# The last half step of a two-stage attention kernel: scalings and copies shared with VectorE, last output tile stored from two queues

## The chip, the cores and the metric

The kernel runs on one core of a Trainium2 chip, as one launch. The metric is the device time of a whole execution in microseconds. Of the core's engines, TensorE (PE) multiplies and transposes, VectorE (DVE), ScalarE (ACT) and GpSimd (POOL) work on tiles in SBUF and PSUM, and SyncE (SP) issues the transfers to and from DRAM, which 16 DMA engines carry out.

## The reference

Two attentions follow each other. The first is a causal window attention of 8 batches, 8 heads, 576 positions and 64 dimensions, with a window of 64. Its output, as 576 rows of 512 per batch, goes into a mixture of 4 attention experts: a gate picks the best two of four experts for every row, each expert has its own query, key, value and output weights, and the outputs are added with the gate's weights.

```python
# stage 1, per batch and head
mask = (rel >= 0) & (rel < window)
scores = np.where(mask, scale * q @ k.T, -1e9)
x = softmax(scores) @ v                        # then heads side by side: x is (8, 576, 512)
# stage 2, for each of 4 experts
q, k, v = x @ wq[e], x @ wk[e], x @ wv[e]      # 512 -> 64
a = softmax(causal(q @ k.T / 8))
ye = a @ v @ wo[e]                             # 64 -> 512
out += mask[..., None] * w[:, :, kk:kk + 1] * ye   # only where e is among the row's best two
```

## The kernel before

Stage 1 works in groups of four 64-row blocks for a pair of heads; stage 2 works per batch b on a pair pr of experts at a time. One (b, pr) is a half step, and there are 16 of them; the two stages overlap, so that stage 2 of a batch runs while stage 1 works on later batches. A list of calls, each with a due time from a table of positions, is sorted by that time and executed in this order when the program is written. For due times from 1.0 to 15.5 TensorE's order is that of the list; behind that, where the last half steps lie, a scheduler orders TensorE's instructions by when their inputs are expected. The instructions of the other engines follow in the order that the scheduler gives them; each engine then works through its own list, and waits on semaphores for the others.

A half step of stage 2 goes like this. TensorE makes the scores, VectorE takes a masked minimum (L471), ScalarE the exponentials (L475). `s2_w` multiplies the unnormalised probabilities by gate weight over row sum: three short VectorE operations (L506 to L508) give a factor for each of nine tiles x = 0 to 8, and GpSimd multiplies the tiles (L512). Tile 0 is `px` (64 columns); tiles 1 to 8 have 192, 192, 320, 320, 448, 448, 576 and 576 columns. Tiles 1 to 4 lie in the buffer named p_0 in the profile; 5 to 8 in p_1 or p_2, depending on pr (p_2 in the last half step). `s2_t` transposes 128-column pieces on TensorE, four to a PSUM tile of the tag "t" (three buffers), in two parts: part 0 from p_0 (k = 0, 1, 2) and part 1 from p_1 or p_2 (k = 0 to 3). In the names of such tiles, t_7_1_0_1 is b = 7, pr = 1, part 0, k = 1. Copies on ScalarE (L528 to L561) bring them into pt_0 or pt_1. `s2_av_mm` multiplies them with the values (L580) into another PSUM tile of the same tag, o_7_1_0 or o_7_1_1, in 36 or 20 products. `s2_av_out` splits the result into a high part yh (ScalarE, L591) and a rest yl (VectorE, L592). `s2_o` multiplies those of both pairs with the output weights: `three` (L340 to L342) is called for each pair, six matmuls of 512 columns for one of five output tiles ops_0 to ops_4 of a batch.

The last step of `s2_o` is the one that ends the program: VectorE copies a tile of 128 x 512 from PSUM into an SBUF tile "out" (two buffers) at L601, and SyncE stores it (L603). The ninth block of 64 rows of an even batch is kept until the odd batch after it: tile j = 4 holds 64 rows of each and is stored by two transfers of 64 rows (L606).

Of the kernel before, what the change touches and what calls it, by code (L numbers as in the profile page):

```python
# [11 lines left out]
AF = mybir.ActivationFunctionType  # L12
OP = mybir.AluOpType
# [3 lines left out]
NB, NH, S, D = 8, 8, 576, 64  # L17
# [22 lines left out]
def window_attention_moe_attention(ctx: ExitStack, tc: tile.TileContext, qT, kT, vW,  # L40
                                   wg, wq, wk, wv, wo, out):
    nc = tc.nc
# [69 lines left out]
    for h in range(2):  # L112
        r = slice(64 * h, 64 * h + 64)
# [12 lines left out]
    for h in range(2):  # L126
        r = slice(64 * h, 64 * h + 64)
        for x in range(2):
            c = slice(64 * x, 64 * x + 64)
# [168 lines left out]
    def row(i, e):  # L298

        return (0, 0, 384, 0, 896)[i] + e * (64 + 128 * i)  # L300

    def chunk(i, e, c):

        if e == 0:
            return row(i, 0) + 128 * c
        return row(i, 1) + 64 + 128 * (i - 1 - c)
# [32 lines left out]
    def three(ps, ah, al, bh, bl, first, last):  # L339
        nc.tensor.matmul(ps, lhsT=ah, rhs=bh, start=first, stop=False)  # L340
        nc.tensor.matmul(ps, lhsT=ah, rhs=bl, start=False, stop=False)  # L341
        nc.tensor.matmul(ps, lhsT=al, rhs=bh, start=False, stop=last)  # L342
# [120 lines left out]
    def s2_soft(b, pr, k):  # L463
# [26 lines left out]
        if k == 1:  # L490
            least(banks[0][:, 448:512], PX[0][:, 0], m_f[:, 1, 64:128], r2[:, 0, 0:1])
            exp(PX[0][:, 0], 0)
            s2_w(b, pr, 0)
        if k == 3:
            nc.vector.tensor_tensor(r2[:, 0, 7:9], m2[:, :, 0], m2[:, :, 1], op=OP.min)  # L495
            for e in range(2):
                exp(P2S[pr][1][:, row(4, e):row(4, e) + 576], 7 + e)
            if pr or b % 2:
                s2_w(b, pr, 1)

    def s2_w(b, pr, k):

        x0, x1 = ((0, 7), (7, 9))[k]
        r2 = R2[b, pr]
        x = slice(x0, x1)
        nc.vector.tensor_scalar_add(r2[:, 2, x], r2[:, 1, x], 1e-9)  # L506
        nc.vector.reciprocal(r2[:, 2, x], r2[:, 2, x])
        nc.vector.tensor_mul(r2[:, 3, x], r2[:, 2, x], G2[b % 2][:, pr, x])  # L508
        for x in range(x0, x1):
            i, e = (x + 1) // 2, (x + 1) % 2  # L510
            p = PX[0][:, 0] if x == 0 else P2S[pr][i > 2][:, row(i, e):row(i, e) + 64 + 128 * i]
            nc.gpsimd.tensor_scalar(p, p, r2[:, 3, x:x + 1], 1.0, op0=OP.mult, op1=OP.mult)  # L512

    def s2_t(b, pr, part, k):
        ps = psum.tile([128, 512], F32, tag="t", bufs=3, name=f"t2_{b}_{pr}_{part}_{k}")
        pt = PT2[part]

        def one(col, i, e, c):

            at = chunk(i, e, c) if c < i else row(i, 1) - 64  # L520
            nc.tensor.transpose(ps[:, col:col + 128], P2S[pr][part][:, at:at + 128], ident)  # L521

        def odd(col, col0):
            for e in range(2):
                r = slice(64 * e, 64 * e + 64)
                dst = pt[r, e, col0:col0 + 256].rearrange("r (a c) -> r a c", c=64)[:, 0:4:3]
                src = ps[r, col:col + 256].rearrange("r (a c) -> r a c", c=64)[:, 1::2]
                nc.scalar.activation(dst, src, AF.Copy)  # L528

        if part == 0 and k == 0:  # L530
            for e in range(2):
                for i in (1, 2):
                    one(256 * e + 128 * i - 128, i, e, 0)
            nc.scalar.activation(pt[:, :, 64:320], ps.rearrange("r (e c) -> r e c", e=2), AF.Copy)
        elif part == 0 and k == 1:
            for e in range(2):
                one(128 * e, 2, e, 1)
            one(256, 1, 0, 1)
            one(384, 2, 0, 2)
            nc.scalar.activation(pt[:, :, 384:512], ps[:, 0:256].rearrange("r (e c) -> r e c", e=2), AF.Copy)  # L540
            odd(256, 320)
        elif part == 0:
            nc.tensor.transpose(ps[:, 0:128], PX[0].rearrange("r a c -> r (a c)"), ident)
            for e in range(2):
                nc.scalar.activation(pt[64 * e:64 * e + 64, e, 0:64], ps[0:64, 64 * e:64 * e + 64], AF.Copy)
        elif k < 2:
            for c in range(2):
                for i in (3, 4):
                    one(256 * c + 128 * i - 384, i, k, c)
            nc.scalar.activation(pt[:, k, 0:512], ps, AF.Copy)  # L550
        elif k == 2:
            for e in range(2):
                for i in (3, 4):
                    one(256 * e + 128 * i - 384, i, e, 2)
            nc.scalar.activation(pt[:, :, 512:768], ps.rearrange("r (e c) -> r e c", e=2), AF.Copy)
        else:
            for e in range(2):
                one(128 * e, 4, e, 3)
            one(256, 3, 0, 3)
            one(384, 4, 0, 4)  # L560
            nc.scalar.activation(pt[:, :, 832:960], ps[:, 0:256].rearrange("r (e c) -> r e c", e=2), AF.Copy)  # L561
            odd(256, 768)

    def y_col(b, blk):

        return 64 * blk + 64 * (b % 2 == 1 and blk == BLK - 1)
# [27 lines left out]
    def s2_o(b, j):  # L594
        ps = psum.tile([128, DM], F32, tag="s", bufs=5, name=f"ops_{b}_{j}")
        for pr in range(2):
            y0 = y_col(b, 2 * j) if j < 4 else 512
            yh, yl = (y[pr][:, y0:y0 + 128] for y in (YH, YL))
            three(ps, yh, yl, whi["o"][:, pr], wlo["o"][:, pr], pr == 0, pr == 1)
        t = work.tile([128, DM], F32, tag="out", bufs=2, name=f"out_{b}_{j}")  # L600
        nc.vector.tensor_copy(t, ps)  # L601
        if j < 4:
            nc.sync.dma_start(out[b, 128 * j:128 * j + 128], t)  # L603
        else:
            for i in range(2):
                nc.sync.dma_start(out[b - 1 + i, 512:576], t[64 * i:64 * i + 64])  # L606

    def half(n):

        it = []  # L610

        def spread(key, calls):
            lo, hi = POS[key + "e" if n >= 2 * NB else key]
            for i, (f, *args) in enumerate(calls):
                it.append((n + lo + (hi - lo) * (i + 0.5) / len(calls), f, args))

        b, pr = (n - 1) // 2, (n - 1) % 2
        zb, zp = (n - 2) // 2, n % 2
        if 0 <= zb < NB and n >= 2:
            late = "l" if zp == 0 and zb % 2 == 0 and MERGE else str(zp)  # L620
            spread("T0" + str(zp), [(s2_t, zb, zp, 0, k) for k in range(3)])
            spread("T1" + late, [(s2_t, zb, zp, 1, k) for k in range(4)])
            if late == "l":
                spread("VT", [(s2_v, zb, 4), (s2_gate, zb, 4, 5), (s2_w, zb, 0, 1)])
            if zp == 1:
                spread("O0", [(s2_o, zb, j) for j in range(2)])
                spread("O1", [(s2_o, zb, j) for j in range(2, 4 + zb % 2)])
        if n >= 1 and b < NB:
            if pr == 0:
                spread("KQ1", [(f, b, 1, h) for h in range(2) for f in (s2_k, s2_q)])  # L630
        if n % 2 == 0 and n // 2 < NB:
            b = n // 2
            spread("V", [(s2_v, b, j) for j in range(5 - MERGE)])
            spread("G", [(s2_gate, b, 0, 4)])
            spread("KQ0", [(f, b, 0, h) for h in range(2) for f in (s2_k, s2_q)])
        return it
# [26 lines left out]
    for g in range(NG1):  # L663
        t = (g - LEAD) / 4.5 + LAG[0]
# [4 lines left out]
        b, k = g // 9, g % 9  # L669
# [72 lines left out]
```

## Time and profile before

| | us |
|---|---|
| three executions | 493.12, 493.98, 496.29 |
| median | 493.98 |
| the profiled execution | 494.57 |
| its span, first to last instruction | 492.5 |
| TensorE busy in it | 475.6 |
| VectorE / ScalarE / GpSimd busy | 391.5 / 345.4 / 201.0 |

In the profile a row of a group names the line, the engine, the operation and out<-in. Buffer numbers are left out there. A chain of waits is followed back from the last instruction: each piece has its start, its length and what ran. "issue" is time for which the profile shows no cause, and names such as DVEq and SPq are the engines' own instruction queues. The windows give busy times between two moments, with the share in which the 16 DMA engines moved data.

### The profile page before, as it was taken

The page shows a single profiled execution, that of the slowest core. Times are in us where ns is not written, and L with a number is a line of the kernel's source. Part 1 is how long each engine was busy: PE and PEld are TensorE (multiplying, and loading weights), DVE is VectorE, ACT ScalarE, POOL GpSimd, SP SyncE. Part 2 cuts the span into 40 slices and gives each one's busy share as a digit, 9 for nine tenths or more (in the row PEclk, how much of TensorE's full clock was granted, in tenths as well). Part 3 has the DMA queues.
Part 4 walks back from the last instruction along what each step waited for, and adds up shares of the span by engine and source line. Part 5 has one row for each costly group of instructions (what it writes and reads, how often), then busy time and mean ns, then how long its engine had stood idle before and what let it go on. Part 6 is the DMA issues. An engine that isn't in the chain of part 4 may idle for free. (4 is left out here: it accounts for less than half of the span.)

```text
span 492.5 us, 14853 instructions
## 1 busy us (share of the span) xinstructions
PE 475.6 (97%) x5132; PEld 443.6 (90%) x5132; DVE 391.5 (79%) x1820; ACT 345.4 (70%) x1365; POOL 201.0 (41%) x545
## 2 busy tenths in 40 slices
PE   5899999999999999999999999999999999999995
PEld 5789999899999999999999999999999999898874
DVE  6767879789978898888987899788997886655533
ACT  5989788677676765858577776667768685556480
POOL 7647254633444262542536243263345413242130
PEclk9999999999999999999999999999999999999999
DMA  8995252321433343223433214433152100200103
GB/s 299 320 217 149 83 158 92 101 78 65 150 94 100 111 129 126 68 77 121 165 101 100 75 70 149 116 100 101 54 169 65 50 23 24 64 3 23 65 1 107
DMA packets 49754, 51.28 MB, mean 104 GB/s; under 512 B 35472, under 2 KB 35984, under 8 KB 49680
## 3 DMA queue, kind: packets, MB, share of 16 engines
q1 hardware_dynamic: 49680, 50.35, 33.3%
q8 instruction: 40, 0.66, 0.6%
q14 instruction: 34, 0.28, 0.2%
HBM read 40.90 MB, written 9.44 MB: 102 GB/s over the span
## 5 line engine op out<-in xcount | busy, mean ns | idle before, releaser
L475 ACT ACTIVATE p<-p,r 128x192 f32<-128x192 f32 (+3 forms) x128 | 77.3, 605 | 47.4 <-DVE r L495 30.8
L512 POOL TENSOR_SCALAR p<-p,r 128x192 f32<-128x192 f32 (+3 forms) x128 | 74.6, 601 | 80.0 <-DVE r L508 50.2
L205 POOL TENSOR_SCALAR p<-p,st 128x64 f32<-128x64 f32 x216 | 65.4, 325 | 64.3 <-PE o L266 19.3
L182 PE MATMUL s<-k,qbd 128*128 128x128 f32 (+1 forms) x540 | 74.6, 284 | 7.9 <-POOL qbd L94 5.7
L200 ACT ACTIVATE p<-p,st 128x64 f32<-128x64 f32 x216 | 72.4, 338 | 13.7 <-DVE p L198 5.9
L182 PEld LDWEIGHTS s<-k,qbd 128*128 128x128 f32 x540 | 68.6, 197 | 10.8 <-POOL qbd L94 5.7
L238 DVE TENSOR_TENSOR pt<-t,tri 64x512 f32<-64x512 f32 (+1 forms) x120 | 76.0, 633 | 2.2
L193 DVE CUSTOM_DVE_ANT_0 sm<-s,win 128x128 f32<-128x128 f32 x264 | 65.3, 284 | 7.5 <-PE s L182 4.5
L471 DVE CUSTOM_DVE_ANT_0 p<-s,causal 128x320 f32<-128x320 f32 (+3 forms) x160 | 66.6, 472 | 0.6
L521 PE MATMUL t<-ident,p 128*128 128x128 f32 x384 | 52.3, 273 | 0.3 <-POOL p L512 0.2
L580 PE MATMUL o<-pt,v 128*64 128x128 f32 (+3 forms) x896 | 49.9, 263 | 0.0
L580 PEld LDWEIGHTS o<-pt,v 128*64 128x64 f32 x896 | 45.3, 137 | 1.7 <-ACT pt L528 0.4
L521 PEld LDWEIGHTS t<-ident,p 128*128 128x128 f32 x384 | 44.0, 141 | 2.1 <-POOL p L512 0.7
L456 PE MATMUL s<-kt,qt 64*128 64x256 f32 (+2 forms) x480 | 44.3, 321 | 0.1
L266 PE MATMUL o<-pt,v 128*64 128x64 f32 x1152 | 41.3, 225 | 1.0 <-ACT pt L227 1.0
L266 PEld LDWEIGHTS o<-pt,v 128*64 128x64 f32 x1152 | 36.5, 138 | 6.1 <-ACT pt L227 1.6
L340 PE MATMUL kps<-xh,wkhi 128*128 128x320 f32 (+1 forms) x128 | 39.3, 307 | 1.7 <-DVE m L471 1.7
L200 ACT ACTIVATION_READ_ACCUMULATOR p<-p,st 128x1 f32 x216 | 40.9, 189 | 0.0
L340 PE MATMUL qps<-xh,wqhi 128*128 128x320 f32 (+1 forms) x128 | 39.9, 311 | 0.0
L340 PE MATMUL v2ps<-wvhi,xh 128*128 128x260 f32 x128 | 38.9, 304 | 0.0
L361 POOL TENSOR_SCALAR v<-vo 64x128 f32<-64x128 f32 x64 | 19.2, 301 | 47.8 <-ACT vo L359 31.7
L456 PEld LDWEIGHTS s<-kt,qt 64*128 64x128 f32 x480 | 34.5, 185 | 4.5 <-DVE r L471 0.5
(141 smaller groups left out, 1238.9 us busy)
## 6 DMA issues: line engine op xcount, KB each, us to landing
v<-in_vW_dram SPq DMA_DIRECT2D x32, 576.0 KB, 5.2
k<-in_kT_dram SPq DMA_DIRECT2D x30, 320.0 KB, 3.9
out_dram<-out SPq DMA_DIRECT2D x32, 256.0 KB, 2.0
qbd<-in_qT_dram SPq DMA_DIRECT2D x56, 144.0 KB, 3.3
out_dram<-out SPq DMA_DIRECT2D x8, 128.0 KB, 2.4
p<-in_kT_dram SPq DMA_DIRECT2D x2, 320.0 KB, 7.3
q<-in_qT_dram SPq DMA_DIRECT2D x2, 288.0 KB, 3.4
p<-in_qT_dram SPq DMA_DIRECT2D x2, 288.0 KB, 7.1
```

The lines of the kernel that those rows point to most:

```text
L182: nc.tensor.matmul(ps[:, i, c:], lhsT=qbd_buf[p % 2][:, b], rhs=pairs[p][1][:, 64 * b + c:64 * b + 128], start=True, stop=True)
L200: nc.scalar.activation(pt[:, i], pt[:, i], AF.Exp, bias=st[:, 0, i:i + 1], scale=-1.0, accum_out=st[:, 1, i:i + 1])
L205: (nc.vector if g < FIRST and i < 1 else nc.gpsimd).tensor_scalar(pt[:, i], pt[:, i], st[:, 2, i:i + 1], 1.0, op0=OP.mult, op1=OP.mult)
L238: nc.vector.tensor_mul(t[64 * w:64 * w + 64, :n, e], ps[r, :n], tri[r, w, None, :].to_broadcast([64, n, 128]))
L266: nc.tensor.matmul(o[64 * h:64 * h + 64, 4 * (k % 2) + i], lhsT=pairs[p][2][:, h, b], rhs=t[:, i, 64 * h:64 * h + 64], start=True, stop=True)
L340: nc.tensor.matmul(ps, lhsT=ah, rhs=bh, start=first, stop=False)
L456: nc.tensor.matmul(banks[e][:, at(i, e):at(i, e) + n], lhsT=QT[pr][r, w, q], rhs=rhs, start=x == 0, stop=x == 2)
L471: nc.vector.tensor_tensor_reduce(out=dst, in0=ps, in1=mask, scale=1.0, scalar=3.0e38, op0=OP.add, op1=OP.min, accum_out=to)
L475: nc.scalar.activation(p, p, AF.Exp, bias=r2[:, 0, x:x + 1], scale=-1.0, accum_out=r2[:, 1, x:x + 1])
L512: nc.gpsimd.tensor_scalar(p, p, r2[:, 3, x:x + 1], 1.0, op0=OP.mult, op1=OP.mult)
L521: nc.tensor.transpose(ps[:, col:col + 128], P2S[pr][part][:, at:at + 128], ident)
L580: nc.tensor.matmul(o[64 * h:64 * h + 64, q0:q0 + w], lhsT=V2[b % 2][:, c, 2 * pr + h], rhs=PT2[part][:, h, x:x + w], start=a == 0, stop=a ...
```

## The change

In the last half step alone, (b, pr) = (7, 1), the tiles with odd x (1, 3, 5 and 7) are scaled by VectorE and not by GpSimd, and the copies of transposes with odd k (k = 1 and 3) are made by VectorE and not by ScalarE, through a helper `copy`. The last output tile (b = 7, j = 4) is copied in two halves of 256 columns: ScalarE takes columns 0 to 255 and issues their store from its own queue, VectorE takes columns 256 to 511 and SyncE issues their store. Each of the two stores covers both batches in one transfer, with a destination of 2 x 64 x 256. Before, each of the two covered one batch with 64 x 512. Lines below the change move by up to 14: L512 is L513 after, L580 is L587, L591 and L592 are L598 and L599, L601 is L615; all copies of transposes have the helper's lines, L521 on VectorE and L523 on ScalarE.

```diff
         for x in range(x0, x1):
...
-            nc.gpsimd.tensor_scalar(p, p, r2[:, 3, x:x + 1], 1.0, op0=OP.mult, op1=OP.mult)
+            engine = nc.vector if (b, pr) == (NB - 1, 1) and x % 2 else nc.gpsimd
+            engine.tensor_scalar(p, p, r2[:, 3, x:x + 1], 1.0, op0=OP.mult, op1=OP.mult)

     def s2_t(b, pr, part, k):
...
+        def copy(dst, src):
+            if (b, pr) == (NB - 1, 1) and k % 2:
+                nc.vector.tensor_copy(dst, src)
+            else:
+                nc.scalar.activation(dst, src, AF.Copy)
+
...
-                nc.scalar.activation(dst, src, AF.Copy)
+                copy(dst, src)
...
-            nc.scalar.activation(pt[:, :, 832:960], ps[:, 0:256].rearrange("r (e c) -> r e c", e=2), AF.Copy)
+            copy(pt[:, :, 832:960], ps[:, 0:256].rearrange("r (e c) -> r e c", e=2))
             odd(256, 768)
...
         t = work.tile([128, DM], F32, tag="out", bufs=2, name=f"out_{b}_{j}")
+        if b == NB - 1 and j == 4:
+            rows = out[b - 1:b + 1, 512:576]
+            nc.scalar.activation(t[:, 0:256], ps[:, 0:256], AF.Copy)
+            nc.scalar.dma_start(rows[:, :, 0:256], t[:, 0:256])
+            nc.vector.tensor_copy(t[:, 256:512], ps[:, 256:512])
+            nc.sync.dma_start(rows[:, :, 256:512], t[:, 256:512])
+            return
         nc.vector.tensor_copy(t, ps)
         if j < 4:
             nc.sync.dma_start(out[b, 128 * j:128 * j + 128], t)
```

How the orders move is shown at three places. The first is VectorE at the last half step's scalings, before; r is the tile of factors, yl the rest of the output of the attention.

```order
1756 L508 TENSOR_TENSOR r_7_1_7750<-r_7_1_7750,g_1_143 128x7
1757 L506 TENSOR_SCALAR r_7_1_7750<-r_7_1_7750 128x2
1758 L507 RECIPROCAL r_7_1_7750<-r_7_1_7750 128x2
1759 L508 TENSOR_TENSOR r_7_1_7750<-r_7_1_7750,g_1_143 128x2
1760 L592 TENSOR_TENSOR yl_138<-o_7_0_1_7848,yh_136 128x192
1761 L592 TENSOR_TENSOR yl_138<-o_7_0_1_7848,yh_136 128x64
1762 L592 TENSOR_TENSOR yl_139<-o_7_1_0_7871,yh_137 128x320
1763 L601 COPY out_0_7940<-ops_0_7933 128x512
```

And after:

```order
1756 L508 TENSOR_TENSOR r_7_1_7750<-r_7_1_7750,g_1_143 128x7
1757 L513 TENSOR_SCALAR p_0_69<-p_0_69,r_7_1_7750 128x192
1758 L513 TENSOR_SCALAR p_0_69<-p_0_69,r_7_1_7750 128x320
1759 L513 TENSOR_SCALAR p_2_71<-p_2_71,r_7_1_7750 128x448
1760 L521 COPY pt_0_130<-t_7_1_0_1_7834 128x2x128
1761 L521 COPY pt_0_130<-t_7_1_0_1_7834 64x2x64 x2
1762 L506 TENSOR_SCALAR r_7_1_7750<-r_7_1_7750 128x2
1763 L507 RECIPROCAL r_7_1_7750<-r_7_1_7750 128x2
1764 L508 TENSOR_TENSOR r_7_1_7750<-r_7_1_7750,g_1_143 128x2
1765 L513 TENSOR_SCALAR p_2_71<-p_2_71,r_7_1_7750 128x576
1766 L599 TENSOR_TENSOR yl_138<-o_7_0_1_7848,yh_136 128x192
```

The scalings of tiles 1, 3 and 5 (L513) and the copies of t_7_1_0_1 (L521) now stand between the factors for the first seven tiles and those for the last two (L506 to L508).

The second place is TensorE around the last attention products, before (o_7_1_1, L580, is the product of part 1; ops_1 and ops_2 are output tiles):

```order
2383 L342 MATMUL ops_0_7933<-wohi,yl_139 128x512
2384 L340 MATMUL ops_1_7943<-wohi,yh_137 128x512
2385 L580 MATMUL o_7_1_1_7910<-pt_1_131,v_1_145 64x64 x2
2386 L580 MATMUL o_7_1_1_7910<-pt_1_131,v_1_145 64x96 x2
2387 L580 MATMUL o_7_1_1_7910<-pt_1_131,v_1_145 64x128 x12
2388 L580 MATMUL o_7_1_1_7910<-pt_1_131,v_1_145 64x96 x2
2389 L341 MATMUL ops_1_7943<-wolo,yh_137 128x512
2390 L342 MATMUL ops_1_7943<-wohi,yl_139 128x512
2391 L340 MATMUL ops_2_7953<-wohi,yh_136 128x512
```

And after:

```order
2383 L342 MATMUL ops_0_7933<-wohi,yl_139 128x512
2384 L340 MATMUL ops_1_7943<-wohi,yh_137 128x512
2385 L341 MATMUL ops_1_7943<-wolo,yh_137 128x512
2386 L587 MATMUL o_7_1_1_7910<-pt_1_131,v_1_145 64x64
2387 L342 MATMUL ops_1_7943<-wohi,yl_139 128x512
2388 L587 MATMUL o_7_1_1_7910<-pt_1_131,v_1_145 64x64
2389 L587 MATMUL o_7_1_1_7910<-pt_1_131,v_1_145 64x96 x2
2390 L587 MATMUL o_7_1_1_7910<-pt_1_131,v_1_145 64x128 x12
2391 L587 MATMUL o_7_1_1_7910<-pt_1_131,v_1_145 64x96 x2
2392 L340 MATMUL ops_2_7953<-wohi,yh_136 128x512
```

The last two matmuls of ops_1 stood behind the products of o_7_1_1; now L341 stands ahead of them and L342 behind the first of them.

The third place is the end of the program with what each instruction waits for. VectorE before:

```order
1772 L601 COPY out_1_7950<-ops_1_7943 128x512 [waits DMAHW2_49,PE_49]
1773 L592 TENSOR_TENSOR yl_139<-o_7_1_1_7910,yh_137 128x64 [waits Activation_49]
1774 L601 COPY out_2_7960<-ops_2_7953 128x512 [waits DMAHW3_49,PE_49]
1775 L601 COPY out_3_7970<-ops_3_7963 128x512 [waits DMAHW4_49,DVE_49,PE_49]
1776 L601 COPY out_4_7980<-ops_4_7973 128x512 [waits DMAHW5_49,DVE_49,PE_49]
```

After, the end of ScalarE's list:

```order
704 L523 ACTIVATE pt_1_131<-t_7_1_1_2_7896 128x2x256 [waits PE_49]
705 L598 ACTIVATE yh_137<-o_7_1_1_7910 128x192 [waits PE_49]
706 L598 ACTIVATE yh_137<-o_7_1_1_7910 128x64 [waits DVE_49]
707 L610 ACTIVATE out_4_7980<-ops_4_7973 128x256 [waits DMAHW3_49,DMAHW4_49,DMAHW2_49,DMAHW5_49,DMAHW1_49,DMAHW6_49,DMAHW0_49,DMAHW7_49,DVE_49,PE_49]
708 L611 DMA out_dram<-out_4_7980 2x64x256 [waits Activation_49]
```

And the end of VectorE's list after:

```order
1781 L599 TENSOR_TENSOR yl_139<-o_7_1_1_7910,yh_137 128x192 [waits Activation_49]
1782 L599 TENSOR_TENSOR yl_139<-o_7_1_1_7910,yh_137 128x64 [waits Activation_49]
1783 L615 COPY out_2_7960<-ops_2_7953 128x512 [waits DMAHW3_49,PE_49]
1784 L615 COPY out_3_7970<-ops_3_7963 128x512 [waits DMAHW4_49,DVE_49,PE_49]
1785 L612 COPY out_4_7980<-ops_4_7973 128x256 [waits DMAHW5_49,Activation_49]
```

VectorE's copy of the second half (L612) waits for a DMA queue and for ScalarE, where its copy of the whole tile waited for a DMA queue, for itself and for TensorE. ScalarE's copy (L610) has taken over the wait for TensorE, and waits for all eight DMA semaphores.

More of the change, by code (lines that the diff above doesn't have):

```diff
@@ L533, in s2_t @@
                     one(256 * e + 128 * i - 128, i, e, 0)
-            nc.scalar.activation(pt[:, :, 64:320], ps.rearrange("r (e c) -> r e c", e=2), AF.Copy)
+            copy(pt[:, :, 64:320], ps.rearrange("r (e c) -> r e c", e=2))
         elif part == 0 and k == 1:
@@ L539, in s2_t @@
             one(384, 2, 0, 2)
-            nc.scalar.activation(pt[:, :, 384:512], ps[:, 0:256].rearrange("r (e c) -> r e c", e=2), AF.Copy)
+            copy(pt[:, :, 384:512], ps[:, 0:256].rearrange("r (e c) -> r e c", e=2))
             odd(256, 320)
@@ L544, in s2_t @@
             for e in range(2):
-                nc.scalar.activation(pt[64 * e:64 * e + 64, e, 0:64], ps[0:64, 64 * e:64 * e + 64], AF.Copy)
+                copy(pt[64 * e:64 * e + 64, e, 0:64], ps[0:64, 64 * e:64 * e + 64])
         elif k < 2:
@@ L549, in s2_t @@
                     one(256 * c + 128 * i - 384, i, k, c)
-            nc.scalar.activation(pt[:, k, 0:512], ps, AF.Copy)
+            copy(pt[:, k, 0:512], ps)
         elif k == 2:
@@ L554, in s2_t @@
                     one(256 * e + 128 * i - 384, i, e, 2)
-            nc.scalar.activation(pt[:, :, 512:768], ps.rearrange("r (e c) -> r e c", e=2), AF.Copy)
+            copy(pt[:, :, 512:768], ps.rearrange("r (e c) -> r e c", e=2))
         else:
```

## Prediction

> **What bounds the kernel now.** I read first the page's busy times, then the chain of waits over the last 23 us, then the windows and groups in which a term of the sum has its price. The busy times of the whole program come first.
>
> ```profile
> span 492.5 us, 14853 instructions
> PE 475.6 (97%) x5132; PEld 443.6 (90%) x5132; DVE 391.5 (79%) x1820; ACT 345.4 (70%) x1365; POOL 201.0 (41%) x545
> ```
>
> TensorE bounds everything up to its last matmul, so work taken from ScalarE or GpSimd pays only where TensorE waits for it. All edits lie in the last half step, (b, pr) = (7, 1). Its chain of waits follows (start, length, what).
>
> ```profile
> 471.19 0.13 DVE r L508
> ...
> 471.50 0.32 POOL px L512
> 471.81 1.82 POOL p L512 x4
> ...
> 473.68 0.98 PE t L521 x7
> 474.66 2.90 PE o L580 x56
> ...
> 478.86 0.87 PE t L521 x8
> ...
> 480.43 2.25 PE o L580 x36
> 482.68 0.43 PE ops L341
> 483.11 0.23 PE ops L342
> ...
> 484.50 0.24 PE ops L342
> ...
> 484.77 0.70 DVE out L601
> 485.49 2.01 DMA out_dram<-out
> ...
> 487.57 0.40 issue
> 487.97 0.69 DVE out L601
> ```
>
> Three places can move: GpSimd's scalings at 471.5 that hold the transposes, the attention products at 480.43 that wait for copies, and everything after the last matmul. That matmul is the first row below; the second holds the two stores of the last tile.
>
> ```profile
> 487.12 0.39 PE L342 MATMUL ops<-wohi,yl 128*128 128x512 f32 x1
> ...
> 488.69 1.11 SPq L606 DMA_DIRECT2D out_dram<-out  x2
> ```
>
> TensorE ends at 487.51, the last copy runs 487.97 to 488.66, SyncE issues until 489.80. What a store takes from issue to landing comes from two questions to the trace, one per line of code: L606 stores 64 rows of 512 (128 KB), L603 128 rows (256 KB). Durations are of the issue itself, in ns (min/median/max).
>
> ```profile
> L606 SPq DMA_DIRECT2D out_dram<-out x8: 473/562/589, 191.7 to 489.2; - x8
> DMA to landing us min/median/max: 2.3/2.4/2.5
> ```
>
> ```profile
> L603 SPq DMA_DIRECT2D out_dram<-out x32: 332/343/509, 114.6 to 486.9; - x32
> DMA to landing us min/median/max: 2.0/2.0/4.3
> ```
>
> The second small store starts at 489.80 - 0.59 = 489.21 and lands 2.4 later, at 491.6; the span closes 0.9 after that. The sum is made on this execution (494.57 us, span 492.5), which lies 0.59 above the median of 493.98; I add the same difference to the median.
>
> **Gate 1, the scalings (L512, after: L513).** Rows for the gate: the transposes' stretches and ScalarE's copies in the timeline, and the groups that price a scaling.
>
> ```profile
> 472.04 1.46 PE L521 MATMUL t<-ident,p 128*128 128x128 f32 x9
> 472.91 1.09 ACT L550 ACTIVATE pt<-t 128x512 f32<-128x512 f32 x2
> 473.68 0.98 PE L521 MATMUL t<-ident,p 128*128 128x128 f32 x7 [0.18 <-POOL p L512]
> 474.55 0.20 ACT L475 ACTIVATION_READ_ACCUMULATOR p<-p,r 128x1 f32 x1
> 480.09 0.56 ACT L528 ACTIVATE pt<-t 64x128 f32<-64x128 f32 x2
> ```
>
> ```profile
> L512 POOL TENSOR_SCALAR p<-p,r 128x320 f32<-128x320 f32 x32 | 16.6, 530 | 0.0
> L512 POOL TENSOR_SCALAR p<-p,r 128x192 f32<-128x192 f32 x32 | 14.9, 479 | 0.0
> L205 POOL TENSOR_SCALAR sm<-sm,st 128x128 f32<-128x128 f32 x54 | 20.7, 399 | 17.7 <-DVE st L203 6.4 <-DVE st L193 5.1 <-ACT sm L200 2.2
> L540 ACT ACTIVATE pt<-t 128x256 f32<-128x256 f32 x16 | 6.1, 382 | 7.5 <-PE t L521 7.5
> L205 DVE TENSOR_SCALAR sm<-sm,st 128x128 f32<-128x128 f32 x18 | 5.3, 296 | 0.2
> L471 DVE CUSTOM_DVE_ANT_0 p<-s,causal 128x320 f32<-128x320 f32 x64 | 29.0, 484 | 0.0
> L471 DVE CUSTOM_DVE_ANT_0 p<-s,causal 128x192 f32<-128x192 f32 x32 | 10.1, 353 | 0.6
> ```
>
> Today GpSimd scales px and then two tiles of 192 and two of 320 columns one after another, and is done with p_0 at 471.81 + 1.82 = 473.63. Afterwards it keeps px, one of 192 and one of 320: 471.50 + 0.32 + 0.48 + 0.53, about 472.8. VectorE takes the other 192 and 320; no row shows its tensor_scalar at these widths. Between its 296 ns at 128 columns and its L471 op at 484 ns for 320, I take the L471 prices: 471.32 + 0.35 + 0.48 = 472.15, which hides beside GpSimd. So p_0 is ready near 472.8. TensorE works on px and eight older transposes (0.87/8 = 0.109 each, by the chain's x8) in the x9 row from 472.04 until about 472.9, so it no longer waits for the scalings. What is late next is a PSUM buffer: four of the eight new transposes go into one that the first L550 copy empties at about 473.5 (the row's two share 1.09). Four at 0.109 plus start-up put the L580 block at about 474.1 instead of 474.6: gain 0.5. Bounds: 0 (the engines disturb each other) and 0.6 (the second L550, at 474.00, must be done before L580 starts).
>
> Two rows early in the trace show what a disturbance looks like.
>
> ```profile
> 36.60 2.10 POOL L205 TENSOR_SCALAR sm<-sm,st 128x128 f32<-128x128 f32 x3 [1.27 <-DVE st L203]
> 36.97 1.23 DVE L162 SCALAR_TENSOR_TENSOR wklo<-pt,wkhi 128x1024 fp32r<-128x1024 f32 x1 [0.25 <-ACT wkhi L161]
> ```
>
> Three GpSimd scalings take 2.10 beside a VectorE op of 1.23, where three at 399 ns are 1.20: one was held for most of VectorE's op. The Trainium skill ("SBUF — State Buffer", section "Who interferes with whom") says that VectorE's tensor_scalar in a two-port mode, or any VectorE op with two SBUF inputs, holds a port pair exclusively against GpSimd. By that rule the new pairs of scalings would run one after another and the 0.5 would be gone; these rows agree for an op with two inputs, and none shows it for tensor_scalar at these widths.
>
> What VectorE now does first delays its own L506 to L508 for the two last scalings; those wait for an exponential that ends at 474.75, when VectorE's 448-column scaling and three copies are over (the transposes are done at 472.9 + 4 x 0.109 = 473.35, and such copies take 0.38 and 0.56 on ScalarE by the rows L540 and L528: about 474.3). These edits cost nothing while that cover stands.
>
> **Gate 2, the copies (L528 to L561, now alternating between ScalarE and VectorE).** The 36 products at 480.43 took 2.25; the 36 products of an earlier step, with nothing to wait for, are the row below. The last copies that the 480.43 block waits for are ScalarE's two at 480.09 above, which end at 480.65.
>
> ```profile
> 455.78 1.91 PE o L580 x36
> ```
>
> With half of the copies on VectorE, the last are done about when TensorE arrives, so up to 2.25 - 1.91 = 0.34 goes. Against it, L342 of ops_1 now sits between two L580 products. In the chain, the one matmul on which TensorE comes from L580 to ops took 0.43 (482.68), the next 0.23: 0.20 for one more such change. I take 0.14, bounds 0 and 0.34. VectorE's copies of out_0 and out_1 move ahead of yl; their stores start later or earlier by tenths, and nobody waits for them. TensorE thus ends 0.5 + 0.14 = 0.64 earlier, at 486.87.
>
> **The last tile.** The change has one wait that the diff does not show: VectorE's half (L612) waits for ScalarE's half (L610), since both write the same tile. Behind L610 only ScalarE's own store is queued, behind L612 only SyncE's waits. ScalarE's half waits for out_2's store, which frees the buffer: 0.64 earlier, it lands at 487.50 - 0.64 = 486.86. From TensorE's end, at the same moment, to the copy the trace has 0.03 (out_2: 484.74 to 484.77) and 0.46 (out_4, 0.40 of it "issue"); I take 0.23. No row has ScalarE copying from this tile; the nearest of the size are L540 above (382 ns) and, for VectorE:
>
> ```profile
> L430 DVE TENSOR_TENSOR qt<-qps,qt 128x256 fp32r<-128x256 f32 x32 | 13.3, 414 | 2.8 <-ACT qt L429 2.3
> ```
>
> ScalarE 487.10 to 487.48, its store issued at 487.50; VectorE until 487.93, SyncE's store issued at 487.95. Before, the issues were at 488.69 and 489.21: 1.25 earlier for the last one, if both stores then took what stores took.
>
> They have another shape: [2][64][256] on the DRAM side, outermost count 2, where all stores of the trace have 64 or 128. How stores use the engines, in two windows (us, five engines' busy time, clock, share of 16 DMA engines, GB/s):
>
> ```profile
> 481.70:482.60 0.90, 0.90 (x19) 0.79 (x15) 0.00 (x0) 0.00 (x0) 0.00 (x0) 1.00 0.78 291
> 489.80:491.30 1.50, 0.00 (x0) 0.00 (x0) 0.00 (x0) 0.00 (x0) 0.00 (x0) 1.00 0.83 175
> ```
>
> The first holds one L603 store: 0.90 x 0.78 x 16 = 11.2 engine-us for 262 KB, 23.3 GB/s per engine. The second holds the two 64-row stores: 19.9 engine-us for 262 KB, 13.2 GB/s per engine. Half the bytes with half the rows land later (2.4) than the whole (2.0), so landing goes by how the outer count spreads rather than by bytes. A store whose outermost count is 2 has, by that reading, two shares: two engines work and fourteen idle. No row shows such a store, so its cost lies between a small store's 2.4 and the one-pair cases below. I take two engines, the same two for both stores, at 23.3 GB/s, since each gets 64 rows in a sequence, closer to the long store's eight than to the short one's four. Fixed part: 2.0 - 11.2/16 = 1.3. Streaming: 262 KB / (2 x 23.3 GB/s) = 5.6. Last landing 487.50 + 1.3 + 5.6 = 494.4, against 491.6: **+2.8**.
>
> The Trainium skill ("DMA: Bandwidth & Descriptors", section "Why a DMA increments its semaphore by 16 and not by 1") lets a transfer use the largest number of engines up to 16 that divides the outermost count of both sides, the lowest-numbered ones. Here that is 2 by both stores on one pair; the trace has no store that could show it.
>
> **The rivals.** *Stores spread over 16 engines as today.* For it: all 40 stores of the trace do. Last landing 487.95 + 2.2 = 490.15, -1.45: 492.5 (491.9 to 493.1 with the gates' bounds). *Two different pairs, side by side.* 487.95 + 1.3 + 2.8 = 492.05, +0.45: 494.4. Against it: two queues do not make two sets of engines in any row. *Slow packets on one pair, the case on the slower side.* Rows of 1 KB could go at the 13.2 GB/s of the second window: 9.9 of streaming, 498.7, +7.1: 501.1. From 7.7 us of streaming on it is over 1% slower. Against it: that window's share is mostly the start and end of four-row pieces. *GpSimd and VectorE block each other*, so that gate 1 gives nothing: forecast + 0.5 = 497.3; the 36.60 row speaks for it.
>
> **How the numbers follow.** Forecast: 493.98 + 2.8 = **496.8**, chance 0.5; its own range 495.3 (5 us of streaming, 0.9 less by bounds and repeats) to 498.3 (no gain at either gate, slower start). Spread stores 0.25, separate pairs 0.08, slow packets 0.05, blocking 0.07, unnamed 0.05. To hold 8 in 10 the range must reach down to the spread case: 491.7 to 498.7; it leaves out the slow packets, the unnamed and some tails. 1%, about what a measurement of this kernel tells from no change, is 489.0 and 498.9: no case lies below (0.01); above lie slow packets and the upper tails of the forecast and of blocking, 0.10; the rest, 0.89, is within.
>
> **What would show it.** Gate 1: the first L587 at about 474.1, no GpSimd wait ahead of the transposes. Gate 2: x36 at about 1.9. Last matmul ending near 486.9. Last tile: L612 starting when L610 ends. Stores: DMA share about 0.12 (2 of 16) at 40 to 50 GB/s for some 5 us after 488.8. Landings 2 to 2.4 after issue with all engines busy would say that I was wrong on the stores; a rate near 26 GB/s, that the packets are slow; GpSimd scalings of a microsecond, that the engines block each other.

## The result, and the profile after

The changed kernel takes 498.17 us (median of 6, 497.68 to 498.84), the kernel before 493.79 (median of 6, 493.12 to 496.29). The ratio is 1.008, with an interval of 1.0055 to 1.0105: 0.8% slower, inside the 1% that the forecast called no change, and 1.4 us above its 496.8, near the upper end of the 495.3 to 498.3 that it gave for this case.

The page's head of the changed kernel's profile (498.58 us):

```profile
span 496.5 us, 14858 instructions
PE 476.1 (96%) x5132; PEld 443.7 (89%) x5132; DVE 395.8 (80%) x1831; ACT 343.9 (69%) x1359; POOL 200.5 (40%) x541
```

Its chain of waits over the last 26 us (start, length, what), without the stretches that are as before:

```profile
470.90 0.36 POOL px L513
...
471.62 2.01 PE t L528 x16
473.64 2.90 PE o L587 x56
...
479.65 0.26 PE o L587 x2
479.90 0.42 PE ops L342
480.33 1.90 PE o L587 x28
482.23 0.43 PE ops L340
...
484.58 2.00 DMA out_dram<-out
...
486.60 0.04 ACTq L610
...
486.68 0.04 ACTq L610
...
486.76 0.04 ACTq L610
...
486.84 0.39 ACT out L610
...
487.26 0.42 DVE out L612
```

GpSimd's scalings are gone from the chain: sixteen transposes now run in one piece and the L587 block begins 2.74 after px where it took 3.16. TensorE ends at 486.60 and VectorE's last copy at 487.68, 0.98 earlier than the 488.66 of before. All of it is lost behind that. The timeline's last two rows are the two issues, the windows show what followed (us, five engines, clock, share of 16 DMA engines, GB/s):

```profile
487.25 1.15 ACTq L611 DMA_DIRECT2D out_dram<-out  x1
487.71 0.63 SPq L613 DMA_DIRECT2D out_dram<-out  x1
```

```profile
488.60:491.10 2.50, 0.00 (x0) 0.00 (x0) 0.00 (x0) 0.00 (x0) 0.00 (x0) 0.50 0.13 33
491.10:492.00 0.90, 0.00 (x0) 0.00 (x0) 0.00 (x0) 0.00 (x0) 0.00 (x0) 0.50 0.13 20
492.00:495.00 3.00, 0.00 (x0) 0.00 (x0) 0.00 (x0) 0.00 (x0) 0.00 (x0) 0.50 0.14 48
```

A DMA share of 0.13 is two engines out of 16. They move 33 GB/s at first, 20 in the 0.9 us in which the first packets of SyncE's store come (from 491.07), and 48 from 492.0 on. In all these seven microseconds no other engine does anything. The trace has the last landings at 493.955 for ScalarE's store, 6.7 after its issue, and at 495.65 for SyncE's, where before all had landed at 491.60. That later landing of 4.05 is the difference of the two profiled times, 4.01.

### The profile page after: what moved, and what is told of

The parts are those of the page before. It is cut to its first block, busy times and chain, and to the rows that moved or that the text cites. A ratio compares the mean times of both kernels' runs of the same rounds, so it can differ in the third digit from the quotient of the medians.

```text
span 496.5 us, 14858 instructions
## 1 busy us (share of the span) xinstructions
PE 476.1 (96%) x5132; PEld 443.7 (89%) x5132; DVE 395.8 (80%) x1831; ACT 343.9 (69%) x1359; POOL 200.5 (40%) x541
## 5 line engine op out<-in xcount | busy, mean ns | idle before, releaser
L513 POOL TENSOR_SCALAR p<-p,r 128x192 f32<-128x192 f32 (+3 forms) x124 | 73.2, 610 | 81.3 <-DVE r L508 52.2
L523 ACT ACTIVATE pt<-t 128x512 f32<-128x512 f32 (+2 forms) x185 | 64.4, 386 | 11.1 <-PE t L528 8.2
L471 DVE CUSTOM_DVE_ANT_0 p<-s,causal 128x320 f32<-128x320 f32 (+3 forms) x160 | 66.6, 472 | 0.5
L587 PE MATMUL o<-pt,v 128*64 128x128 f32 (+3 forms) x896 | 50.0, 262 | 0.0
L587 PEld LDWEIGHTS o<-pt,v 128*64 128x64 f32 x896 | 45.3, 137 | 1.7 <-ACT pt L523 0.5
L456 PE MATMUL s<-kt,qt 64*128 64x256 f32 (+2 forms) x480 | 44.2, 320 | 0.1
L340 PE MATMUL kps<-xh,wkhi 128*128 128x320 f32 (+1 forms) x128 | 39.3, 307 | 1.8 <-DVE m L471 1.8
L340 PE MATMUL qps<-xh,wqhi 128*128 128x320 f32 (+1 forms) x128 | 39.8, 311 | 0.0
L340 PE MATMUL v2ps<-wvhi,xh 128*128 128x260 f32 x128 | 38.9, 304 | 0.0
```

Source lines behind the costliest of these rows:

```text
L471: nc.vector.tensor_tensor_reduce(out=dst, in0=ps, in1=mask, scale=1.0, scalar=3.0e38, op0=OP.add, op1=OP.min, accum_out=to)
L513: engine.tensor_scalar(p, p, r2[:, 3, x:x + 1], 1.0, op0=OP.mult, op1=OP.mult)
L587: nc.tensor.matmul(o[64 * h:64 * h + 64, q0:q0 + w], lhsT=V2[b % 2][:, c, 2 * pr + h], rhs=PT2[part][:, h, x:x + w], start=a == 0, stop=a ...
```

## The experiments

The theory is that a store gets only as many DMA engines as its outermost count allows, two here, and that sharing the work with VectorE gains some tenths. One rival says that ScalarE's queue, used here for the first time, or its rows of 1 KB are what is slow; another that the two engines get in each other's way. For reading the rest, one table gives four stretches of the traced executions: from the start of L508 to the L580 (L587) block, from there to TensorE's end, from there to the first store of the last tile, and to the last landing. They are worked out from the traces' starts and landings.

| run | L508 to L580 | to TensorE's end | to the first issue | TensorE's end to last landing |
|---|---|---|---|---|
| before | 3.45 | 12.92 | 1.18 | 4.09 |
| the change | 3.03 | 13.04 | 0.65 | 9.05 |
| share_only | 3.02 | 13.06 | 0.82 | 3.72 |
| scal_only | 3.01 | 12.92 | 0.83 | 3.75 |
| copies_only | 3.45 | 13.06 | 0.81 | 3.72 |
| tail_only | 3.45 | 12.92 | 0.66 | 9.03 |
| one_queue | 3.01 | 13.06 | 0.65 | 8.41 |
| one_transfer | 3.02 | 13.05 | 0.82 | 8.72 |
| four_stores | 3.02 | 13.06 | 0.64 | 3.67 |
| split_tiles | 3.02 | 13.04 | 0.45 | 3.49 |
| rows_two_queues | 3.01 | 12.91 | 0.76 | 3.40 |
| scal_split | 3.02 | 12.92 | 0.45 | 3.49 |
| scal_again | 3.02 | 12.94 | 0.81 | 3.70 |

The parts add up: whoever shares the scalings gains 0.43, whoever shares the copies loses 0.13, and whoever stores with an outermost count of 2 loses about 5. The start of the last half step itself, up to which all of these kernels do the same, lay between 469.7 and 471.4 in these executions, so that a single execution's time doesn't show the tenths. The copy of out_4 before began 0.46 after TensorE's end, in other executions of that tail about 0.1: its 4.09 has some 0.35 that belong to this one execution.

### The sharing alone

The last tile as before, the rest of the change kept:

```diff
-        if b == NB - 1 and j == 4:
-            rows = out[b - 1:b + 1, 512:576]
...
-            return
```

> The shared scalings and copies stay, the last tile is copied and stored as before. If the whole loss lies in the two new stores (theory 1), the end comes back to its old shape: last TensorE matmul about 0.3 earlier relative to the first factors (0.42 from gate 1, -0.11 from gate 2, as the changed kernel's trace has them), time 493.5, ratio 0.999. If the sharing itself costs (theory 2, VectorE and GpSimd in each other's way), the time is above 494.5.

493.93 us against 494.01, ratio 0.9995 (0.9976 to 1.0014): the loss is gone, and the gain of 0.3 is too small to be timed. Of the chain of waits of this run:

```profile
471.78 0.36 POOL px L513
...
474.51 2.90 PE o L587 x56
...
484.76 0.70 DVE out L608
```

2.73 and 10.25, as in the changed kernel: sharing costs nothing on balance, so the rival that has VectorE and GpSimd blocking each other falls as the cause of the loss.

### The last tile alone

The kernel before with the changed `s2_o` only:

```diff
         t = work.tile([128, DM], F32, tag="out", bufs=2, name=f"out_{b}_{j}")
+        if b == NB - 1 and j == 4:
+            rows = out[b - 1:b + 1, 512:576]
...
+            return
```

> Only the last tile is changed. Theory 1: last landing about 8.4 us after ScalarE's store is issued, as in the changed kernel, against 2.9 from first issue to last landing before; with 0.5 less between TensorE's end and the first issue that is +4.9 us: 498.7. Theory 2: the tail is worth less than half of the loss, below 496.

498.70 us, ratio 1.0111 (1.0085 to 1.0137), as theory 1 had it. The first issue comes 0.66 after TensorE's end, the last landing 9.03 after it. All of the loss is here.

### The same bytes and queues with an outermost count of 64

```diff
-            rows = out[b - 1:b + 1, 512:576]
...
-            nc.scalar.dma_start(rows[:, :, 0:256], t[:, 0:256])
+            for i in range(2):
+                nc.scalar.dma_start(out[b - 1 + i, 512:576, 0:256], t[64 * i:64 * i + 64, 0:256])
...
-            nc.sync.dma_start(rows[:, :, 256:512], t[:, 256:512])
+            for i in range(2):
+                nc.sync.dma_start(out[b - 1 + i, 512:576, 256:512], t[64 * i:64 * i + 64, 256:512])
```

> As the changed kernel, but each half of the last tile is stored by two transfers of 64 x 256 (outermost count 64), ScalarE's half from its queue and SyncE's from its. Theory 1 (the outermost count of 2 leaves two engines): the stores spread over 16 engines, land 2.3 to 2.6 after the last issue (some 488.3 on the changed kernel's clock), so the last landing is about 490.8 and the time about 493.3, 4.9 under the changed kernel. Rival (ScalarE's queue is slow, or rows of 1 KB are): the same bytes in the same rows from the same queues keep most of the loss, above 496.

493.33 us, ratio 0.9988 (0.9974 to 1.0003). ScalarE's stores in the trace, by their line:

```profile
L611 ACTq DMA_DIRECT2D out_dram<-out x2: 556/583/610, 486.6 to 487.1; - x2
...
DMA to landing us min/median/max: 2.0/2.0/2.1
```

ScalarE's queue and rows of 1 KB land after 2.0 us: neither of them was slow. What differs is that each store's outermost count is 64. There are also four transfers now and not two; that this isn't the reason is shown by one_transfer and early_counts below.

### Both stores from one queue

```diff
-            nc.scalar.dma_start(rows[:, :, 0:256], t[:, 0:256])
+            nc.sync.dma_start(rows[:, :, 0:256], t[:, 0:256])
```

> As the changed kernel, but both 2 x 64 x 256 stores are issued by SyncE. Theory 1: still two engines, so 5.6 us of streaming at 46 ns per KB and engine stay: the time is within 1.6 us of the changed kernel (496.6 to 498.6), lower if the 1.5 us of stalls in its stream come from two queues taking turns on the same engines. Rival (ScalarE's queue is what is slow): the last landing is 3 us or less after the last issue, time below 494.5.

498.02 us, ratio 1.0091 (1.0074 to 1.0107). The last landing is at 495.12, 7.76 after the first issue of this row, where two queues took 8.40:

```profile
487.36 0.62 SPq L611 DMA_DIRECT2D out_dram<-out  x1
```

The windows of this run, cut where the slow stretch ends:

```profile
488.60:491.00 2.40, 0.00 (x0) 0.00 (x0) 0.00 (x0) 0.00 (x0) 0.00 (x0) 1.00 0.13 32
491.00:494.50 3.50, 0.00 (x0) 0.00 (x0) 0.00 (x0) 0.00 (x0) 0.00 (x0) 0.62 0.14 49
```

Two engines again, and the slow beginning is there with one queue. The second slow stretch of the changed kernel, 20 GB/s from 491.1 to 492.0, is not: it comes where SyncE's packets join ScalarE's (tail_only has one too, 24 GB/s from 491.3 to 492.4). Once both queues take turns, from 492.0 on, the two engines move 48. So the second queue costs about 0.6 (8.40 - 7.76, one execution each), of which that stretch is 0.9 x (1 - 20/48) = 0.5; the slow beginning is the greater part of what the stream loses.

### One transfer of 2 x 64 x 512

With the sharing kept, VectorE copies the whole tile and SyncE stores it at once:

```diff
             for i in range(2):
-                nc.sync.dma_start(out[b - 1 + i, 512:576], t[64 * i:64 * i + 64])
+                if b < NB - 1:
+                    nc.sync.dma_start(out[b - 1 + i, 512:576], t[64 * i:64 * i + 64])
+            if b == NB - 1:
+                nc.sync.dma_start(out[b - 1:b + 1, 512:576], t)
```

> Sharing kept; the last tile is copied whole by VectorE and stored by SyncE in one transfer of 2 x 64 x 512: outermost count 2, rows of 2 KB, one queue, half as many rows. Theory 1 (two engines whatever the row size): about 1.3 + 5.4 = 6.7 us from issue to landing, if the slow stretch at the start of the stream goes with the number of rows, 7.4 if it goes with the transfer; time 497 to 498. Rival (it is the rows of 1 KB, or two transfers in flight, that are slow): 4 us or less, time below 495.5.

498.47 us, ratio 1.0094 (1.0068 to 1.0119). Issued at 487.23, landed at 495.13: 7.90. Theory 1 holds on the two engines, with half as many rows of twice the size; the slow beginning doesn't get shorter with fewer rows, and the 7.4 was too low; so was the time expected, 497 to 498. On each engine most packets take 0.084; in the first 2.5 us pauses of 0.1 to 0.3 come at the start and after every fourth packet, and there are hardly any behind that. What causes them stays open.

### Other outermost counts, in the middle of the program

The kernel before, with the earlier pair tiles cut otherwise:

```diff
+            if b == 3:
+                nc.sync.dma_start(out[b - 1:b + 1, 512:576], t)
+                return
             for i in range(2):
-                nc.sync.dma_start(out[b - 1 + i, 512:576], t[64 * i:64 * i + 64])
+                cut = {1: (60, 56), 5: (62, 61)}.get(b, (64, 64))[i]
+                nc.sync.dma_start(out[b - 1 + i, 512:512 + cut], t[64 * i:64 * i + cut])
+                if cut < 64:
+                    nc.sync.dma_start(out[b - 1 + i, 512 + cut:576], t[64 * i + cut:64 * i + 64])
```

> The kernel before, with the stores of the three earlier pair tiles cut otherwise, where nothing at the end waits for them: b = 1 in 60 + 4 and 56 + 8 rows, b = 3 in one transfer of 2 x 64 rows, b = 5 in 62 + 2 and 61 + 3 rows (512 columns each; the last tile as before). Theory 1 (a store gets as many DMA engines, up to 16, as divide its outermost count): 60 rows go to 15 engines and 56 to 14, landing 2.3 to 2.8 us after issue; 62 rows to 2 engines, 31 rows of 2 KB each at 84 ns, 1.3 + 2.6 = 3.9 us and up to 2 more of slow stretch; 61 rows to one engine, 1.3 + 5.1 = 6.4 us or more; 2 x 64 to 2 engines, 7.9 us as in one_transfer. Rival (only the nested pattern of two blocks is slow): 62 and 61 rows land after 2.3 to 2.8 us like 60. Time of the kernel within 1 us of before, since no engine waits for these stores at the end.

The trace has a landing mark for each engine of a store. A store over all engines that nothing holds up shows 16 marks within 0.3 us; each of the nine here shows one mark some 0.4 to 1.0 us after its issue and then as many as are listed here:

```
outermost count   60   56    8    4   2x64   62    61     3     2
later marks       15   14    8    4     2     2     1     3     2
issue to last     1.89 1.82 1.49 1.42  8.28  5.15  9.03  8.93  5.01   us
```

The largest number up to 16 that divides the count fits all nine: 62 rows go to two engines and 61 to a single one, while 60 go to 15. The rival, that only the nested pattern is slow, falls. (3 and 2 rows landed right behind 61 and 62, which fits small counts on the same first engines.) The single engine shows itself too. In this window only the 61 rows were still being moved, and its DMA share is one engine of 16 (TensorE works for a quarter of it):

```profile
430.20:434.30 4.10, 1.03 (x10) 0.56 (x6) 0.00 (x0) 0.00 (x0) 0.00 (x0) 0.91 0.07 26
```

Of the sizes, 60 and 56 rows landed sooner than expected; 62 took 5.15, within the 3.9 and up to 2 more, and 61 took 9.03, far above the 6.4 that were named as its least. Stores over all 16 engines issued behind a slow one waited for its engines: the 128 rows issued at 308.38 behind 2x64 had 14 marks by 312.62 and the last two at 315.62 and 316.01, 7.6 after the issue, where such stores take 2.0. Of the 128 rows issued behind the 61, at 426.21, one mark came last, at 435.10.

And the last sentence of the expectation was wrong: this kernel took 506.15 us in a single execution, 12 us above before. From the waits of this run (who waited for what, us in total, times, longest):

```profile
DVE out L601 <- DMA out_dram<-out: 11.6, 2, 5.9
```

"out" has two buffers, so a later copy on VectorE waits for the slow store, and what is queued behind it (TensorE's L340 and L456, by the same trace) waits with it. Two such waits, 11.6 in all, are about what was lost.

### Which part of the sharing gains

Only the scalings, and only the copies, each with the old tail:

```diff
-            if (b, pr) == (NB - 1, 1) and k % 2:
+            if False:
```

> Only the scalings are shared; all copies of transposes are on ScalarE and the last tile is as before. Theory 1 (gate 1 alone gives the 0.42, and the loss of 0.1 to 0.13 at gate 2 comes from the order of TensorE that the shared copies bring): from GpSimd's first scaling to the start of the L587 block 2.7 us (before 3.16), from there to the copy of out_2 10.1 us as before (share_only 10.25); time 493.5, 0.1 under share_only, which no timing here resolves. Rival (the copies on VectorE are needed for gate 1): the start of the block moves by 0.1 or less.

```diff
-            engine = nc.vector if (b, pr) == (NB - 1, 1) and x % 2 else nc.gpsimd
+            engine = nc.gpsimd
```

> Only the copies are shared; scalings on GpSimd and the last tile as before. Theory 1: no gain at gate 1 (3.1 to 3.2 us from GpSimd's first scaling to the L587 block) and 10.2 us from there to the copy of out_2, so a loss of about 0.1. Rival: gate 2's 36 products fall to 1.9 with nothing lost at the crossings, 9.8 to 9.9 us.

The chains of waits, scal_only first, then copies_only:

```profile
470.71 0.36 POOL px L513
...
473.44 2.90 PE o L587 x56
...
479.22 2.24 PE o L587 x31
...
483.55 0.70 DVE out L608
```

```profile
471.18 0.32 POOL px L513
...
474.35 2.90 PE o L587 x56
...
480.35 0.26 PE o L587 x2
...
481.04 1.90 PE o L587 x29
...
484.58 0.70 DVE out L608
```

2.73 and 10.11 with the scalings, 3.17 and 10.23 with the copies, as theory 1 expected. The copies do take the wait out of the products, but TensorE's order that comes with them cuts the 36 in two (2.24 becomes 0.26 + 1.90) and puts L342 between, at 0.43 instead of 0.23.

scal_only took 493.04 us, ratio 0.9967 (0.9955 to 0.998), which is 1.6 us where its trace accounts for 0.4; copies_only took 493.85 in a single execution. The first was therefore timed anew, and beside it a kernel with the best of the parts:

> The same kernel as scal_only, timed anew on whichever chip comes. Its 0.9967 is 1.6 us, of which the trace of the last 25 us explains 0.4. Theory 1 (0.4 is all there is, the rest is which executions were drawn): ratio 0.998 to 1.000. Rival (something before the last half step is faster too): 0.9955 to 0.998 again.

493.35 us, ratio 0.9975 (0.9957 to 0.9993). Faster than before in both, by a little, but the interval reaches into both expectations, and the four stretches of its trace are those of scal_only to within 0.05; whether more than 0.4 us is gained, and where, stays open.

### Where the wait between the halves comes from, and a better tail

```diff
+        if b == NB - 1 and j == 4:
+            u = work.tile([128, 256], F32, tag="outa", bufs=1, name="out_a")
+            w = work.tile([128, 256], F32, tag="outv", bufs=1, name="out_v")
+            nc.scalar.activation(u, ps[:, 0:256], AF.Copy)
+            nc.vector.tensor_copy(w, ps[:, 256:512])
+            for i in range(2):
+                nc.scalar.dma_start(out[b - 1 + i, 512:576, 0:256], u[64 * i:64 * i + 64])
+                nc.sync.dma_start(out[b - 1 + i, 512:576, 256:512], w[64 * i:64 * i + 64])
+            return
         t = work.tile([128, DM], F32, tag="out", bufs=2, name=f"out_{b}_{j}")
...
```

> Sharing kept; each half of the last tile gets an SBUF tile of its own and two stores of 64 x 256, ScalarE's from its queue, VectorE's from SyncE's. Theory 1 (what makes VectorE's half wait for ScalarE's is the PSUM tile that both read, not the SBUF tile that both write): VectorE's copy still starts when ScalarE's ends, and ScalarE's starts 0.05 to 0.1 after TensorE's end, not 0.24, since it no longer waits for a store; last landing about 3.5 after TensorE's end (four_stores 3.68). Rival (the shared SBUF tile is the cause): the two copies overlap, the last landing comes 0.4 earlier still, 3.1.

The end of its chain:

```profile
486.40 0.25 PE ops L342
486.65 0.02 issue
486.68 0.39 ACT out_a L610
487.07 0.02 issue
487.09 0.42 DVE out_v L611
```

The two copies still follow each other though no SBUF tile is shared: the trace has VectorE's copy waiting for ScalarE's, and what the two still share is the PSUM tile that both read. Whether the chip would let them run side by side no run shows; the program has the wait in it. ScalarE starts 0.03 after TensorE, where three waits (ACTq L610 in the chain of the changed kernel) took 0.24: its tile is new, and no store has to free it. The last landing is 3.49 after TensorE's end; the time is 493.02, ratio 0.9992 (0.9976 to 1.0008).

In rows_two_queues only the scalings are shared, and the tile is copied whole, into a buffer of its own, and stored by rows, one transfer from each queue:

```diff
+        last = b == NB - 1 and j == 4
+        t = work.tile([128, DM], F32, tag="outl" if last else "out", bufs=1 if last else 2, name=f"out_{b}_{j}")
...
-                nc.sync.dma_start(out[b - 1 + i, 512:576], t[64 * i:64 * i + 64])
+                (nc.scalar if last and i else nc.sync).dma_start(out[b - 1 + i, 512:576], t[64 * i:64 * i + 64])
```

> Scalings shared, copies on ScalarE, the last tile copied whole by VectorE into a buffer of its own, one 64 x 512 store issued by SyncE and the other by ScalarE. If both queues feed 16 engines without hindering each other, the two issues start together and the last landing is about 3.1 us after TensorE's end (share_only 3.73, before 4.09); with gate 1's 0.42 the time is 492.8, ratio 0.998. If ScalarE's queue is slower to start (its issues took 0.55 and 1.15), the gain is 0.4 or less.

3.40 from TensorE's end to the last landing, 0.3 more than expected: SyncE's store landed 2.33 after its issue, ScalarE's 2.64. That is the expectation's second case, a gain of 0.4 or less: 0.3 against the 3.72 of share_only. 493.56 us against the 492.8 expected, ratio 0.9989 (0.9972 to 1.0007).

The last kernel puts the scalings of scal_only together with the tail of split_tiles:

> Scalings shared, copies of transposes on ScalarE, and the last tile in two SBUF tiles with four 64 x 256 stores from two queues. By the single traces: gate 1 0.42 earlier, no loss at gate 2, last landing 3.47 after TensorE's end where the old tail took 3.73 to 4.09: 0.7 to 1.0 us under before, ratio 0.998. It should be level with scal_again within 0.3 us.

493.11 us, ratio 0.9985 (0.9964 to 1.0005), level with scal_again. Its trace has both gains, 3.02 and 12.92 and 3.49, but no timing here separates the versions without the two-engine stores from each other.

## Why the prediction was right, and where it was off

**The stores.** The step that decided, an outermost count of 2 on two engines, the same two for both stores, is shown by the DMA share of 0.13, by two late landing marks per store, by four_stores, which keeps bytes, rows and queues, and by the nine counts of early_counts. The size was off: from ScalarE's issue to the last landing 6.9 were forecast (1.3 fixed and 5.6 of streaming), and 8.40 measured. ScalarE's first packet starts at 488.55, 1.30 after the issue, and the last packet ends at 495.33, 0.32 before the last landing. So the fixed part is 1.6, and the streaming, the mis-sized term, took 6.8. The 23.3 GB/s per engine is met only in the later part (48/2 = 24); the first 2.5 us run at 33/2 = 16.5, and the 0.9 in which the second queue's packets join at 10. The row of 13.2 GB/s was put aside as the start and end of short pieces. The packets in the trace say otherwise: those of the two 64-row stores took 0.153 on average, those of an L603 store of the same row size 0.087. These short stores were slow packet by packet; whether that is the same thing as the slow beginning stays open.

**The hint was weaker than its use.** I argued that landing goes by the outer count because 64 rows land after 2.4 and 128 after 2.0. Both go to 16 engines, and 60 or 56 rows on 15 or 14 landed sooner, after 1.9 and 1.8. That pair of rows says nothing on the number of engines, so going by it alone the conclusion was luck. By the rule of the Trainium skill that was cited there ("DMA: Bandwidth & Descriptors", "Why a DMA increments its semaphore by 16 and not by 1"), the numbers of engines come out as measured in all nine counts, 62 and 61 among them.

**Gate 1.** 0.43 measured, 0.5 forecast. The stretch is now bound by what was named as late next: TensorE's wait there is for ScalarE's copies, as the third row below has it. The pricing by L471 was too dear for VectorE, whose first three scalings (192, 320 and 448 columns) took 1.22 together; GpSimd's got a little longer. The last pair is where both start together:

```profile
470.74 1.22 DVE L513 TENSOR_SCALAR p<-p,r 128x192 f32<-128x192 f32 x3
...
471.22 1.75 POOL L513 TENSOR_SCALAR p<-p,r 128x192 f32<-128x192 f32 x3
...
472.98 0.42 PEld L528 LDWEIGHTS t<-ident,p 128*128 128x128 f32 x4 [0.20 <-ACT pt L523]
...
474.80 0.52 DVE L513 TENSOR_SCALAR p<-p,r 128x576 f32<-128x576 f32 x1
474.93 1.00 POOL L513 TENSOR_SCALAR p<-p,r 128x576 f32<-128x576 f32 x1 [1.96 <-DVE r L508]
```

In the timeline of before, where GpSimd scaled both alone, the two took 1.46:

```profile
475.51 1.46 POOL L512 TENSOR_SCALAR p<-p,r 128x576 f32<-128x576 f32 x2 [0.67 <-ACT pt L528]
```

GpSimd's 576 columns took 1.00 beside VectorE, and about 0.74 alone. So the exclusive port pair that the Trainium skill describes ("SBUF — State Buffer", "Who interferes with whom") may be what this is, but only 0.26 of it shows: GpSimd started 0.13 into VectorE's 0.52 and ended at 475.93, earlier than the 476.06 that a start behind VectorE and 0.74 give. VectorE paid as well: its 448 columns, begun at 471.34 while GpSimd's first 192 were running, took 0.61, more than its 576 did later. All ten traces with shared scalings have these times to within 0.01. A GpSimd scaling of a microsecond was named as the sign of blocking, and it came; but TensorE reaches the transposes behind it at 476.46, when it is over, and the rival built on it, that the gain would be eaten, did not come true.

**Gate 2.** The sign was wrong: 0.14 gain forecast, 0.13 loss measured in every kernel with shared copies. The step that failed is the price of TensorE's new order. I counted one more crossing between the two kinds of matmul, at 0.20; the order cost 0.45. L342 takes 0.42 instead of 0.23, which is the 0.20. The other 0.26 are the two products ahead of it, for the 34 left take 1.90, as long as 36 without a wait (1.91). The trace's starts tell why: the undisturbed 36 run as two rows of 18 side by side, a pair starting within 0.01 of each other about every 0.1. The two ahead started one behind the other (479.576 and 479.683), so they were of one row, and the 18 of the other were still to come: 1.725 from first to last start in both steps. The wait that the copies took away was worth 0.34, so 0.11 is lost.

**From TensorE's end to the first issue** 0.63 was forecast and 0.65 measured, with the copies of 0.39 and 0.42 at 0.382 and 0.414. The reason given for the wait between the halves, the tile that both write, was wrong: with tiles of their own they still follow each other, and what is left is the PSUM tile (split_tiles). That 0.23 was right for the step from TensorE's end to ScalarE's copy is luck: it was taken halfway between two waits of VectorE, and ScalarE's 0.24 is made of three waits in a row.

Sum of the profiled execution: -0.60 from the start of the half step, which is chance, -0.42 and +0.12 at the gates where -0.5 and -0.14 were forecast, and +4.96 from TensorE's end to the last landing (9.05 - 4.09) where the forecast had +3.44 (494.4 - 486.87 - 4.09). Together that is +4.06 against +2.8; the medians differ by 4.4. Of the rivals, spread stores is what four_stores does (493.33; 492.5 was worked out for that case), and slow packets came true in part, for the first 2.5 us of the stream.

## What to carry to other kernels

Before joining two stores into one, look at the outermost count of the pattern that results: two blocks of 64 rows in one transfer took 7.9 us where two transfers of 64 rows took 2.4 each, and a count such as 62 or 61 is as bad. A store that nobody seems to wait for still holds its buffer, and with two buffers a slow one stopped VectorE for 5.9 us in the middle of the program. When an edit shifts work to another engine, read also what it does to the order of a third one: here the copies were taken out of TensorE's way and the order that came with it gave more back.

## What the hardware showed beyond that

A stream on two DMA engines began slowly here: 16 GB/s per engine for about 2.5 us, with pauses mostly after every fourth packet, and 24 GB/s afterwards, with rows of 1 KB and of 2 KB alike. Where a second queue's packets joined on the same two engines, they fell to 10 GB/s each for 0.9 us. ScalarE's single issue of 2 x 64 x 256 occupied its queue for 1.15 us and SyncE's of the same shape for 0.63; with 64 x 256 both took 0.47 to 0.61.
